# Attention followed by a mixture of experts: a hand-ordered attention phase, and mixing matmuls that write PSUM with a stride

## The chip, the cores and the metric

One core of one Trainium2 chip runs the whole program. The metric is the device time of one execution in microseconds (us), the median of three runs; a profile was taken of one further execution. Five engines work side by side: TensorE (PE, with its weight loads, PEld), VectorE (DVE), ScalarE (ACT), GpSimd (POOL) and SyncE (SP). POOL, SP and ACT also start DMA transfers.

## The reference, cut to what matters

```
P = sort_net                                  # [4, 8, 8, 8]; five row/column normalisations with exp
for _ in range(5):
    P = exp(P - max(P)); P = P / sum_rows; P = P / sum_cols
k_sorted = einsum('bhij,bhjcd->bhicd', P, k_blocks)   # 8 blocks of 96 rows, head size 64
v_sorted = einsum('bhij,bhjcd->bhicd', P, v_blocks)
x = softmax(q_block @ k_sorted_block.T / 8) @ v_sorted_block   # per block of 96 rows
logits = x @ w_gate + modality_bias[modality_id]       # x is [3072, 512], 8 experts
e = argmax(logits); gate = softmax(logits)[e]
out = gate * (relu(x @ w1[e]) @ w2[e])
```

q, k and v are [4, 8, 768, 64]; w1 is [8, 512, 1024] and w2 [8, 1024, 512], all float32 in memory and cast to bf16 by the DMA that loads them.

## The kernel before

The 32 pairs of batch and head are worked in two groups g of 16. In each group a partition holds one (head, block) pair, so that mixing the blocks by P is a matmul of a 128 x 128 slice of k or v with a block-diagonal matrix made of P (`bdk`, `bdv`). `sort_k` mixes 8 of the 96 key rows at a time (12 chunks a group), `sort_v` 4 of the 64 value columns (16 chunks a group); a chunk fills one PSUM bank with 512 float32 a partition, and one copy on DVE or ACT (L168, L175) casts it to bf16 and puts it into `kTb` (a part of `w_all`) or `v_sb`. There are two such banks (`mipsum`), which the q transposes share. In SBUF the mixed k is kept with the row c innermost, the mixed v with the column d innermost, while the chunk in PSUM has c or d outermost, so the copy writes single bf16 elements 192 or 130 bytes apart.

Group 0 is mixed first; then a loop over 32 units u (half a group's blocks of one head) does `expo(u)` on ACT, the scores matmuls of unit u+1, and `av(u)`, which ends on DVE with the normalised rows in `xb`. The 28 chunks of group 1 are mixed in units 2 to 15. Every eighth unit, 12 DMAs on SP's queue store `xb` to `x_scratch`. The order on each engine is made by a scheduler, which may move work that is written later ahead of work written earlier.

The tile `w_all` holds all eight experts' weights, 16 transfers of 1 MB on POOL's queue. Its regions for experts 3 to 7 first serve q, the mixed k, v and k, so a weight transfer has to wait until attention is done with its region.

After the loop comes the gate phase, 24 tiles of 128 rows (L333 to L367): ACT loads a tile of x, PE and DVE work out logits and ranks, ACT copies eight counts into `cnt_sb` (three buffers), and POOL's queue stores them to `cnt_scratch`. Then a short chain of small transfers makes offsets, 24 indirect DMAs scatter the row numbers (L434), and 31 slots run the expert matmuls (L443 to L484). One more transfer matters below: SP's `sidx_scratch<-dummy_t`, which fills a table with 3968 entries of 8 bytes as soon as DVE has set `dummy_t`.

Of the kernel before, what the change touches and what calls it, by code (L numbers as in the profile page):

```python
# [17 lines left out]
def kernel(  # L18
# [13 lines left out]
    nc = tc.nc  # L32
# [28 lines left out]
    KCH = 6  # L61
    KCW = BLK // KCH

    def load_k(g):
        for kc in range(KCH):
            raw = apool.tile([128, KCW * D], BF16, tag="k_raw", name=f"k_raw{g}_{kc}", bufs=2)
            nc.gpsimd.dma_start(out=raw, in_=k_src[g * 128:(g + 1) * 128, kc * KCW * D:(kc + 1) * KCW * D])
            rv = raw.rearrange("p (c d) -> p c d", d=D)
            for par in range(2):
                rows = slice(par * 64, (par + 1) * 64)  # L70
                nc.vector.tensor_copy(k_il[rows, kc * KCW:(kc + 1) * KCW, par], rv[rows])

# [3 lines left out]
    wpool = ctx.enter_context(tc.tile_pool(name="wpool", bufs=1))  # L76
    ph1 = ExitStack()
    apool = ph1.enter_context(tc.tile_pool(name="apool", bufs=3))
# [3 lines left out]
    mipsum = ph1.enter_context(tc.psum_pool(name="mipsum", bufs=2))  # L82

    P_t = singles.tile([BH, NB, NB], FP32)
    nc.sync.dma_start(out=P_t, in_=sort_net.rearrange("b h i j -> (b h) i j"))
    nc.vector.memset(k_il[0:64, :, 1], 0.0)
    nc.vector.memset(k_il[64:128, :, 0], 0.0)
    load_k(0)
    load_v(0)
    q_tiles = {}  # L90

    def load_q(g, hq):
        t = apool.tile([128, 2, 2, 6 * D], BF16, tag="q_in", name=f"q_in{g}_{hq}", bufs=2)
# [3 lines left out]
        il = apool.tile([128, 2, 6, 2, D], BF16, tag="q_il", name=f"q_il{g}_{hq}", bufs=2)  # L97
        for z in range(2):
            nc.vector.tensor_copy(il[:, z], t[:, :, z].rearrange("p r (t d) -> p t r d", d=D))
        q_tiles[g, hq] = il  # L100

    load_q(0, 0)
    load_q(0, 1)

    nc.vector.memset(v_in[:, BLK * D:128 * D], 0.0)
    v_sb = [a1.tile([128, 128, D + 1], BF16, tag=f"v_sb{gg}", name=f"v_sb{gg}") for gg in range(2)]
    for gg in range(2):
        nc.gpsimd.memset(v_sb[gg][:, :, D:D + 1], 1.0)
    attnT = [a1.tile([96, 8 * BLK + 32], BF16, tag=f"attnT{z}", name=f"attnT{z}") for z in range(3)]
    for z in range(3):  # L110
        nc.gpsimd.memset(attnT[z][:, 8 * BLK:], 0.0)
    ident = singles.tile([128, 128], BF16)
    make_identity(nc, ident)
# [4 lines left out]
    P_bf = singles.tile([BH, NB, NB], BF16)  # L118
    for it in range(5):
# [3 lines left out]
        nc.scalar.activation(P_t, P_t, ACT.Exp)  # L123
        nc.vector.tensor_reduce(red, P_t, AX.X, ALU.add)
# [8 lines left out]
    id3 = ident.rearrange("p (a j) -> p a j", j=NB)  # L133
    id3s = bass.AP(tensor=ident.tensor, offset=ident.offset,
                   ap=[ident.ap[0], [1, NB], [NB, 16]])
    jmask = singles.tile([128, NB], FP32)
    nc.vector.tensor_reduce(jmask, id3s, AX.X, ALU.add)
    bmask = singles.tile([128, 16], FP32)
    nc.vector.tensor_reduce(bmask, id3, AX.X, ALU.add)
    bd_v, bd_k = [], []  # L140
    for g in range(2):
        sel = singles.tile([BH, 16, NB], BF16, tag=f"sel{g}", name=f"sel{g}")
        nc.vector.tensor_copy(sel, ident[0:BH, g * 16:(g + 1) * 16].broadcast_to([BH, 16, NB]))
        rep = mipsum.tile([128, NB, NB], FP32, tag="mi", name=f"rep{g}")
        nc.tensor.matmul(rep.rearrange("p a b -> p (a b)"), sel.rearrange("p a b -> p (a b)"),
# [14 lines left out]

    v_cols = v_in.rearrange("p (c d) -> p d c", d=D)

    def sort_k(g, ch, act):
        acc = mipsum.tile([128, 8, 64], FP32, tag="mi", name=f"ka{g}_{ch}")
        for z in range(8):
            nc.tensor.matmul(acc[:, z], k_il[:, ch * 8 + z].rearrange("p r d -> p (r d)"), bd_k[g], start=True, stop=True)  # L166
        dst = kTb[g].rearrange("p (x c) -> p c x", c=BLK)[:, ch * 8:(ch + 1) * 8]
        (nc.scalar.copy if act else nc.vector.tensor_copy)(dst, acc)  # L168

    def sort_v(g, ch, act):  # L170
        acc = mipsum.tile([128, 4, 128], FP32, tag="mi", name=f"va{g}_{ch}")
# [12 lines left out]

# [66 lines left out]
    WLOAD = {14: 0, 18: 1, 22: 2}  # L251
# [62 lines left out]
    for e in range(3, E):  # L314
# [200 lines left out]
```

## Time and profile before

| | |
|---|---|
| Median of three runs | 630.01 us (629.17 to 630.42) |
| Profiled execution, its own time | 628.43 us |
| Span from first to last instruction in it | 626.3 us |
| Mean granted TensorE clock | 0.997 |
| Busy: PE, DVE, ACT, POOL | 277.0, 261.8, 192.7, 137.3 us |
| Loads from HBM, stores | 59.83 MB, 11.33 MB |

The span is shorter than the execution's own time by 2.1 us, which lie before the first and after the last instruction. Busy shares are averages over stages that have different limits, so each stage is read by itself below.

### The profile page before, as it was taken

To read this page: it belongs to the slowest core of one execution; us is meant where nothing else is said; L and a number is where in the kernel's file an instruction comes from. 1 tells how busy PE (TensorE), PEld (TensorE's weight loads), DVE (VectorE), ACT (ScalarE), POOL (GpSimd) and SP (SyncE) were. 2 spreads that over 40 slices of the span, in tenths; PEclk is the share of its full clock that TensorE was granted. 3 is DMA by queue.
4 is the path that set the end of the run, shared out by engine and by line. 5 is a ranking of instruction groups with operands and counts; after the bars stand their busy time and mean duration, and the time that the engine had idled before them with its cause. 6 is when DMAs were issued, how large, how long until landed. Compare 5 with 4: busy or idle time off the path is not lost.

```text
span 626.3 us, 6878 instructions
## 1 busy us (share of the span) xinstructions
PE 277.0 (44%) x2026; PEld 157.8 (25%) x2044; DVE 261.8 (42%) x769; ACT 192.7 (31%) x431; POOL 137.3 (22%) x180
## 2 busy tenths in 40 slices
PE   0002327653754406551000000068787886787775
PEld 0002225542532203331000000023333333333332
DVE  4438888878743506553000000023444343433342
ACT  0006775787332205551000000023333332333222
POOL 5311102110000101222222222122332332223222
PEclk9999999999999999999999999999999998999999
DMA  7999858793826593210000000011121121211210
GB/s 141 119 121 204 140 83 152 117 196 58 136 51 112 83 201 81 59 40 1 7 0 0 0 0 0 0 42 52 51 69 58 50 76 35 68 51 52 46 17 10
DMA packets 41337, 43.56 MB, mean 70 GB/s; under 512 B 14396, under 2 KB 32869, under 8 KB 41046
## 3 DMA queue, kind: packets, MB, share of 16 engines
q0 software_dynamic: 25184, 36.72, 31.6%
q1 hardware_dynamic: 12662, 3.26, 3.4%
q10 hardware_dynamic: 3456, 3.15, 2.2%
q8 instruction: 18, 0.29, 0.2%
q14 instruction: 17, 0.14, 0.1%
HBM read 59.83 MB, written 11.33 MB: 114 GB/s over the span
## 4 chain that ended last, share of the span: by engine, by line
DMA 29%; PE 27%; issue 16%; DVE 15%; ACT 8%; POOL 3%; SPq 1%; POOLq 0%; DVEq 0%; ACTq 0%
DMA sidx_scratch<-rg_all,dest_i_all 12%; PE h_p L462 8%; PE y_p L477 7%; DMA x_scratch<-xb 4%; PE hT_p L473 3%; ACT v_sb L175 3%; DVE v_sb L175 3%; DVE y_sb L481 3%; DMA x_t<-x_scratch,idxg 3%; DVE w_all L168 3%; DMA k_raw<-in_k_dram 3%; DMA q_in<-in_q_dram 2%; ACT w_all L168 2%; DMA out_dram<-y_sb,idxg 2%; PE va L173 2%
## 5 line engine op out<-in xcount | busy, mean ns | idle before, releaser
L456 PE MATMUL xT_p<-ident,x_t 128*128 128x128 bf16 x124 | 21.3, 221 | 141.2 <-DMA x_t<-x_scratch,idxg 123.4
L477 PE MATMUL y_p<-w_all,hT 128*128 x237 | 73.2, 379 | 0.6 <-ACT hT L474 0.6
L457 ACT COPY xT<-xT_p 128x128 bf16<-128x128 bf16 x62 | 16.5, 266 | 167.4 <-PE xT_p L456 167.4
L462 PE MATMUL h_p<-w_all,xT 128*128 x241 | 60.4, 391 | 9.9 <-issue 9.6
L450 POOL DMA_INDIRECT x_t<-x_scratch,idxg x31 | 30.5, 983 | 133.1 <-PE h_p L462 50.9
L457 DVE COPY xT<-xT_p 128x128 bf16<-128x128 bf16 x62 | 11.5, 217 | 111.3 <-PE xT_p L456 111.2
L473 PE MATMUL hT_p<-ident,h_sb 128*128 128x128 bf16 x248 | 49.6, 221 | 10.7 <-DVE hT L474 9.6
L474 DVE COPY hT<-hT_p 128x128 bf16<-128x128 bf16 x124 | 27.9, 225 | 46.6 <-PE hT_p L473 42.0
L456 PEld LDWEIGHTS <-x_t 128*128 128x128 bf16 x124 | 9.8, 97 | 144.1 <-DMA x_t<-x_scratch,idxg 127.0
L175 DVE CAST v_sb<-va 96x512 bf16<-96x512 f32 x16 | 39.1, 2445 | 10.2 <-PE va L173 10.1
L175 ACT CAST v_sb<-va 96x512 bf16<-96x512 f32 x16 | 39.3, 2454 | 12.5 <-PE va L173 12.5
L474 ACT COPY hT<-hT_p 128x128 bf16<-128x128 bf16 x124 | 32.8, 264 | 29.8 <-PE hT_p L473 26.1
L219 ACT ACTIVATE attnT<-sc 96x768 bf16<-96x768 f32 x32 | 26.8, 841 | 48.9 <-PE op L232 39.1
L467 DVE TENSOR_SCALAR h_sb<-h_p 128x512 bf16<-128x512 f32 x31 | 21.4, 692 | 47.5 <-PE h_p L462 47.5
L434 POOL DMA_INDIRECT sidx_scratch<-rg_all,dest_i_all x24 | 23.4, 974 | 75.7 <-DMA sidx_scratch<-rg_all,dest_i_all 71.3
L469 ACT ACTIVATE h_sb<-h_p 128x512 bf16<-128x512 f32 x31 | 18.5, 597 | 63.8 <-PE h_p L462 58.5
L482 POOL DMA_INDIRECT out_dram<-y_sb,idxg x31 | 31.4, 1014 | 25.9 <-DVE xT L457 13.2
L462 PEld LDWEIGHTS <-xT 128*128 128x128 bf16 x248 | 24.7, 99 | 46.3 <-issue 25.7
L168 ACT CAST w_all<-ka 128x512 bf16<-128x512 f32 x12 | 32.5, 2712 | 8.3 <-PE ka L166 8.3
L477 PEld LDWEIGHTS <-hT 128*128 128x128 bf16 x248 | 23.9, 96 | 44.0 <-issue 16.5
L481 DVE TENSOR_SCALAR y_sb<-y_p,idxg 128x512 f32<-128x512 f32 x31 | 23.3, 751 | 27.3 <-PE y_p L477 26.4
L236 DVE TENSOR_TENSOR xb<-op,rs 96x256 bf16<-96x256 f32 x64 | 26.0, 417 | 18.5 <-DMA x_scratch<-xb 16.9
(126 smaller groups left out, 450.4 us busy)
## 6 DMA issues: line engine op xcount, KB each, us to landing
w_all<-in_moe_w_dram POOLq DMA_DIRECT2D x16, 1024.0 KB, 12.2
k_raw<-in_k_dram POOLq DMA_DIRECT2D x12, 256.0 KB, 7.7
w_all<-in_v_dram POOLq DMA_DIRECT2D x2, 1536.0 KB
q_in<-in_q_dram POOLq DMA_DIRECT2D x16, 192.0 KB, 7.5
x_scratch<-xb SPq DMA_DIRECT2D x48, 64.0 KB, 6.1
x_t<-x_scratch ACTq DMA_DIRECT2D x24, 128.0 KB, 2.4
idxg<-sidx_scratch SPq DMA_DIRECT2D x31, 1.0 KB, 1.7
x_t<-x_scratch,idxg POOLq DMA_INDIRECT x31
```

The costliest lines, as they stand in the source:

```text
L168: (nc.scalar.copy if act else nc.vector.tensor_copy)(dst, acc)
L175: (nc.scalar.copy if act else nc.vector.tensor_copy)(dst, acc[0:BLK])
L219: nc.scalar.activation(attnT[u % 3][:, 0:8 * BLK].rearrange("p (r f) -> p r f", r=2), sc_tiles.pop(u)[0:BLK, :, 0:4 * BLK], ACT.Exp, scale ...
L450: nc.gpsimd.indirect_dma_start(out=x_t, out_offset=None, in_=x_dram, in_offset=bass.IndirectOffsetOnAxis(ap=idx[:, :1], axis=0))
L456: nc.tensor.transpose(xT_p, x_t[:, c * 128:(c + 1) * 128], ident)
L457: (nc.scalar.copy if c % 2 else nc.vector.tensor_copy)(xT[:, c], xT_p)
L462: nc.tensor.matmul(h_p, xT[:, c], w_all[:, bass.ds(e_sv * WCOL + c * F + half * 512, 512)], start=(c == 0), stop=(c == 3))
L473: nc.tensor.transpose(hT_p, h_sb[:, fc * 128:(fc + 1) * 128], ident)
L474: (nc.scalar.copy if fc % 2 else nc.vector.tensor_copy)(hT[:, fc], hT_p)
L477: nc.tensor.matmul(y_p, hT[:, fc], w_all[:, bass.ds(e_sv * WCOL + 4 * F + fc * Dm, Dm)], start=(fc == 0), stop=(fc == 7))
L481: nc.vector.tensor_scalar(y_sb, y_p, gate_t[:, 0:1], None, ALU.mult)
L482: nc.gpsimd.indirect_dma_start(out=out, out_offset=bass.IndirectOffsetOnAxis(ap=idx[:, :1], axis=0), in_=y_sb, in_offset=None, bounds_chec ...
```

## The change

The phase up to the end of the loop is put under `tc.manual_schedule()`, so that its instructions stay in the order in which they are written; later code may still be moved forward between them. The written order is new. `sort_k` and `sort_v` let each matmul write every 8th (or 4th) float32 of its bank, so that the copy reads PSUM in order and writes runs of 8 (or 4) bf16, 16 (or 8) bytes. A row of `v_sb` grows from 65 to 72 elements. k is loaded in three pieces, into the tile that later holds the mixed v of group 1, and half of the spreading of k and one clearing of it go from DVE to POOL. All copies of group 1 go to ACT. x gets two buffers, in the region of expert 2, whose weights move behind the loop. The masks are made inside the normalisation.

```diff
+    VW = D + 8
+    order = ExitStack()
+    order.enter_context(tc.manual_schedule())
+    k_raw = v_sb[1].rearrange("p x d -> p (x d)")[:, 0:BLK * D]
...
+    def spread_k(kc, par):
+        eng = nc.gpsimd if par else nc.vector
+        eng.tensor_copy(k_il[rows, kc * KCW:(kc + 1) * KCW, par],
+                        k_raw[rows, cs].rearrange("p (c d) -> p c d", d=D))
...
-        acc = mipsum.tile([128, 8, 64], FP32, tag="mi", name=f"ka{g}_{ch}")
+        acc = mipsum.tile([128, 64, 8], FP32, tag="mi", name=f"ka{g}_{ch}")
         for z in range(8):
-            nc.tensor.matmul(acc[:, z], k_il[:, ch * 8 + z].rearrange("p r d -> p (r d)"), bd_k[g], start=True, stop=True)
-        dst = kTb[g].rearrange("p (x c) -> p c x", c=BLK)[:, ch * 8:(ch + 1) * 8]
+            nc.tensor.matmul(acc[:, :, z], k_il[:, ch * 8 + z].rearrange("p r d -> p (r d)"), bd_k[g], start=True, stop=True)
+        dst = kTb[g].rearrange("p (x c) -> p x c", c=BLK)[:, :, ch * 8:(ch + 1) * 8]
...
-        acc = mipsum.tile([128, 4, 128], FP32, tag="mi", name=f"va{g}_{ch}")
+        acc = mipsum.tile([128, 128, 4], FP32, tag="mi", name=f"va{g}_{ch}")
         for z in range(4):
-            nc.tensor.matmul(acc[:, z], v_cols[:, ch * 4 + z], bd_v[g], start=True, stop=True)
-        dst = v_sb[g].rearrange("p x d -> p d x")[0:BLK, ch * 4:(ch + 1) * 4]
+            nc.tensor.matmul(acc[:, :, z], v_cols[:, ch * 4 + z], bd_v[g], start=True, stop=True)
+        dst = v_sb[g][0:BLK, :, ch * 4:(ch + 1) * 4]
...
     for n, (f, g, ch) in enumerate(sort_jobs[0]):
         f(g, ch, n % 2)
+        if n == 11:
+            load_k(1)
+            make_bd(1)
+    load_v(1)
+    load_q(0, 2)
+    load_q(0, 3)
...
-            x_tiles[g, hf] = apool.tile([BLK, 2, 4, H, D], BF16, tag="xb", name=f"xb{g}_{hf}", bufs=1)
+            x0 = 2 * WCOL + hf * 8 * Dm
+            x_tiles[g, hf] = w_all[0:BLK, x0:x0 + 8 * Dm].rearrange("p (r i h d) -> p r i h d", r=2, i=4, h=H)
...
-    WLOAD = {14: 0, 18: 1, 22: 2}
+    WLOAD = {14: 0, 19: 1}
...
         expo(u)
-        n = u + 1
-        if n < 32:
-            if (n // 8) % 2 == 0:
-                trans_q(n // 16, n % 8)
-            scores(n)
-        av(u)
-        if u >= 2 and u < 16:
+        if u + 1 < 32:
+            scores(u + 1)
+        prep_q(u + 2)
+        if u >= 2:
             for z in range(2):
                 if pend:
                     f, g, ch = pend.pop(0)
-                    f(g, ch, z)
+                    f(g, ch, 1)
+        av(u)
+    order.close()
     ph1.close()
-    for e in range(3, E):
+    for e in range(2, E):
         load_weights(e)
```

The first place is DVE where `dummy_t` is set, the tile that SP's fill of `sidx_scratch` waits for. Before, it stands ahead of the second of five normalisation sums (`red<-P_t`):

```order
L143 COPY sel_189<-ident 32x128
L263 TENSOR_TENSOR biasd<-biasd,bias_419 128x8
L267 MEMSET ones_col 128x1
L269 MEMSET dummy_t 128x62
L275 MEMSET zero_t 1x512
L270 MEMSET dummy_t 128x31
L71 COPY w_all<-k_raw_2_89 64x16x64 x2
L124 TENSOR_REDUCE red<-P_t 32x8
```

Now it stands behind DVE's last copy of group 0's mixed v (`va0_14`) and ahead of the first q tile:

```order
L196 CAST v_sb0_79<-va0_14_388 96x128x4
L288 TENSOR_TENSOR biasd_411<-biasd_411,bias0_409 128x8
L292 MEMSET ones_col_419 128x1
L294 MEMSET dummy_t_421 128x62
L295 MEMSET dummy_t_421 128x31
L300 MEMSET zero_t_425 1x512
L110 COPY q_il0_0_434<-q_in0_0_96 128x768 x2
```

The fill has moved from the normalisation to the end of group 0's mixing, which is also where POOL starts the load of group 1's v.

The second place is ACT in the loop, in units 3 to 5 (`sc` are scores, `ka1` chunks of group 1's k). Before, ACT has one chunk a unit and DVE the other:

```order
L219 ACTIVATE attnT0_123<-sc3_576 96x768
L168 CAST w_all_58<-ka1_1_611 128x8x64
L219 ACTIVATE attnT1_124<-sc4_630 96x768
L168 CAST w_all_58<-ka1_3_665 128x8x64
L219 ACTIVATE attnT2_125<-sc5_684 96x768
L168 CAST w_all_58<-ka1_5_719 128x8x64
```

Now ACT has both:

```order
L243 ACTIVATE attnT0_81<-sc3_540 96x768
L188 CAST w_all_58<-ka1_2_615 128x64x8
L188 CAST w_all_58<-ka1_3_625 128x64x8
L243 ACTIVATE attnT1_82<-sc4_598 96x768
L188 CAST w_all_58<-ka1_4_672 128x64x8
L188 CAST w_all_58<-ka1_5_682 128x64x8
```

DVE has no copy of group 1's chunks left.

The third place is POOL between the last weight transfers and the gate phase's count stores. Before:

```order
L253 DMA w_all<-in_moe_w_dram 128x4x1024
L397 IOTA iota_s 8x31
L367 DMA cnt_scratch<-cnt_sb 8x1x1 x24
L370 DMA cnt_2782<-cnt_scratch 24x8
L395 DMA padT_scratch<-padT_sb 8x1x1
```

Now two weight transfers, those of expert 2, stand behind the iota (which waits for the end of the loop), still ahead of the counts:

```order
L278 DMA w_all<-in_moe_w_dram 128x4x1024
L428 IOTA iota_s 8x31
L278 DMA w_all<-in_moe_w_dram 128x4x1024
L280 DMA w_all<-in_moe_w_dram 128x8x512
L398 DMA cnt_scratch<-cnt_sb 8x1x1 x24
L401 DMA cnt_2751<-cnt_scratch 24x8
```

Both before and now all 16 weight transfers stand ahead of the counts in POOL's queue.

## Rows read from the trace of the kernel before

**Rows 1.** The page, 40 slices of 15.7 us: busy tenths of the DMA engines.
```profile
DMA  7999858793826593210000000011121121211210
```

**Rows 2.** Chain of waits, 0 to 100 us: start us, length us, what.
```profile
24.73 15.69 DMA k_raw<-in_k_dram
...
49.36 0.62 PE ka L166 x8
...
71.67 2.43 DVE v_sb L175
...
74.76 2.43 DVE v_sb L175
...
96.78 1.46 PE tq L194 x12
```

**Rows 3.** Groups by line, 0 to 345 us: busy us, mean ns; idle ahead.
```profile
L175 DVE CAST v_sb<-va 96x512 bf16<-96x512 f32 x16 | 39.1, 2445 | 10.2 <-PE va L173 10.1
...
L168 DVE CAST w_all<-ka 128x512 bf16<-128x512 f32 x12 | 32.5, 2710 | 1.9 <-PE ka L166 1.8
```

**Rows 4.** Timeline of the loop, 188 to 207 us: start us, us, engine, line.
```profile
188.61 0.81 ACT L219 ACTIVATE attnT<-sc 96x768 bf16<-96x768 f32 x1 [0.83 <-PE op L232]
...
190.29 0.81 ACT L219 ACTIVATE attnT<-sc 96x768 bf16<-96x768 f32 x1 [0.88 <-PE op L232]
...
206.21 0.75 DVE L236 TENSOR_TENSOR xb<-op,rs 96x256 bf16<-96x256 f32 x2 [10.85 <-DMA x_scratch<-xb]
```

**Rows 5.** Timeline of POOL in the gate phase: 4th and 24th count store.
```profile
243.66 0.51 POOL L367 DMA_DIRECT2D cnt_scratch<-cnt_sb  x1 [1.58 <-ACT cnt_sb L366]
...
287.97 0.50 POOL L367 DMA_DIRECT2D cnt_scratch<-cnt_sb  x1 [1.38 <-ACT cnt_sb L366]
```

**Rows 6.** The page's costliest groups: two PSUM copies that write 512 elements in order.
```profile
L467 DVE TENSOR_SCALAR h_sb<-h_p 128x512 bf16<-128x512 f32 x31 | 21.4, 692 | 47.5 <-PE h_p L462 47.5
...
L469 ACT ACTIVATE h_sb<-h_p 128x512 bf16<-128x512 f32 x31 | 18.5, 597 | 63.8 <-PE h_p L462 58.5
```

**Rows 7.** Timeline of PE: k mixing, q transposes, an expert's 512-column matmuls.
```profile
63.41 1.01 PE L166 MATMUL ka<-bdk,w_all 128*128 128x64 bf16 x16 [2.38 <-DVE w_all L168]
...
98.69 0.82 PE L194 MATMUL tq<-ident,q_il 128*128 128x128 bf16 x6
...
426.68 1.89 PE L462 MATMUL h_p<-w_all,xT 128*128 x8 [0.28 <-issue]
```

**Rows 8.** Timeline of POOL at the start: clearing, and four load issues.
```profile
0.34 0.12 POOL L499 MEMSET const-uint8-127<- 128x1 uint8 x1
...
3.09 2.89 POOL L95 DMA_DIRECT2D q_in<-in_q_dram  x4
...
7.13 0.30 POOL masks.py:197 MEMSET ident<- 128x128 bf16 x1
```

**Rows 9.** DMA issues: count, KB each, median us from issue to landing.
```profile
w_all<-in_moe_w_dram POOLq DMA_DIRECT2D x16, 1024.0 KB, 12.2
k_raw<-in_k_dram POOLq DMA_DIRECT2D x12, 256.0 KB, 7.7
w_all<-in_v_dram POOLq DMA_DIRECT2D x2, 1536.0 KB
q_in<-in_q_dram POOLq DMA_DIRECT2D x16, 192.0 KB, 7.5
x_scratch<-xb SPq DMA_DIRECT2D x48, 64.0 KB, 6.1
...
sidx_scratch<-dummy_t SPq DMA_DIRECT2D x1, 31.0 KB, 16.2
```

**Rows 10.** Stretches of 6 us: busy PE, PEld, DVE, ACT, POOL; clock, DMA share, GB/s.
```profile
30.00:36.00 6.00, 0.00 (x0) 0.00 (x0) 0.00 (x0) 0.00 (x0) 0.00 (x0) 1.00 1.24 19
...
54.00:60.00 6.00, 1.01 (x16) 0.90 (x16) 5.71 (x4) 5.26 (x2) 1.67 (x3) 1.00 1.13 212
...
90.00:96.00 6.00, 2.26 (x16) 1.70 (x15) 4.84 (x4) 4.66 (x3) 0.58 (x1) 1.00 0.00 0
```

More of the change, by code (lines that the diff above doesn't have):

```diff
@@ L60 @@
     v_src = v.rearrange("b h (n c) d -> (b h n) (c d)", n=NB)
-    KCH = 6
+    KCH = 3
     KCW = BLK // KCH
[L64 to L71, printed above, removed]
-    def load_v(g):
-        nc.gpsimd.dma_start(out=v_in[:, 0:BLK * D], in_=v_src[g * 128:(g + 1) * 128])
+    VW = D + 8
     wpool = ctx.enter_context(tc.tile_pool(name="wpool", bufs=1))
     ph1 = ExitStack()
-    apool = ph1.enter_context(tc.tile_pool(name="apool", bufs=3))
+    apool = ph1.enter_context(tc.tile_pool(name="apool", bufs=2))
     a1 = ph1.enter_context(tc.tile_pool(name="a1", bufs=1))
@@ L96, in load_q, with spread_q @@
                                 .rearrange("h (p t) d -> p h (t d)", t=6))
-        il = apool.tile([128, 2, 6, 2, D], BF16, tag="q_il", name=f"q_il{g}_{hq}", bufs=2)
+        q_raw[g, hq] = t
+    def spread_q(g, hq):
+        t = q_raw.pop((g, hq))
+        il = apool.tile([128, 2, 6, 2, D], BF16, tag="q_il", name=f"q_il{g}_{hq}")
         for z in range(2):
@@ L100, in load_q @@
         q_tiles[g, hq] = il
+    nc.vector.memset(k_il[0:64, :, 1], 0.0)
+    make_identity(nc, ident)
+    load_k(0)
+    load_v(0)
     load_q(0, 0)
     load_q(0, 1)
[L105 to L109, printed above, removed]
+    nc.gpsimd.memset(k_il[64:128, :, 0], 0.0)
+    nc.gpsimd.memset(v_in[:, BLK * D:128 * D], 0.0)
+    for kc in range(KCH):
+        spread_k(kc, 1)
+    nc.gpsimd.memset(v_sb[0][:, :, D:D + 1], 1.0)
     for z in range(3):
         nc.gpsimd.memset(attnT[z][:, 8 * BLK:], 0.0)
-    ident = singles.tile([128, 128], BF16)
-    make_identity(nc, ident)
+    jmask = singles.tile([128, NB], FP32)
+    bmask = singles.tile([128, 16], FP32)
+    sel = [singles.tile([BH, 16, NB], BF16, tag=f"sel{g}", name=f"sel{g}") for g in range(2)]
     red = singles.tile([BH, NB], FP32)
@@ L123 @@
         nc.scalar.activation(P_t, P_t, ACT.Exp)
+        if it == 0:
+            nc.vector.tensor_reduce(jmask, id3s, AX.X, ALU.add)
+        elif it == 1:
+            nc.vector.tensor_reduce(bmask, id3, AX.X, ALU.add)
+            for g in range(2):
+                nc.vector.tensor_copy(sel[g], ident[0:BH, g * 16:(g + 1) * 16].broadcast_to([BH, 16, NB]))
+        else:
+            spread_k(it - 2, 0)
         nc.vector.tensor_reduce(red, P_t, AX.X, ALU.add)
@@ L131, with make_bd @@
         nc.vector.tensor_tensor(P_bf if it == 4 else P_t, P_t, colb, ALU.mult)
[L133 to L139, printed above, removed]
     bd_v, bd_k = [], []
-    for g in range(2):
-        sel = singles.tile([BH, 16, NB], BF16, tag=f"sel{g}", name=f"sel{g}")
-        nc.vector.tensor_copy(sel, ident[0:BH, g * 16:(g + 1) * 16].broadcast_to([BH, 16, NB]))
+    def make_bd(g):
         rep = mipsum.tile([128, NB, NB], FP32, tag="mi", name=f"rep{g}")
-        nc.tensor.matmul(rep.rearrange("p a b -> p (a b)"), sel.rearrange("p a b -> p (a b)"),
+        nc.tensor.matmul(rep.rearrange("p a b -> p (a b)"), sel[g].rearrange("p a b -> p (a b)"),
                          P_bf.rearrange("p a b -> p (a b)"), start=True, stop=True)
@@ L285, with prep_q @@
     mod_words = mod_h.bitcast(I32).ap().rearrange("(t w) -> t w", w=256)
-    load_q(0, 2)
-    load_q(0, 3)
-    trans_q(0, 0)
+    def prep_q(u):
+        if u < 32 and (u // 8) % 2 == 0:
+            if u % 2 == 0:
+                spread_q(u // 16, (u % 8) // 2)
+            trans_q(u // 16, u % 8)
+    prep_q(0)
+    prep_q(1)
     scores(0)
@@ L293 @@
     for u in range(32):
-        if u == 0:
-            load_k(1)
-            load_v(1)
+        if u < 3:
+            spread_k(u, 1)
+            spread_k(u, 0)
+        if u == 3:
+            nc.gpsimd.memset(v_sb[1][:, :, D:D + 1], 1.0)
         if 9 <= u <= 12:
```

37 lines of the change are left out of this document (24 added, 13 removed).

## The prediction

> **What bounds the kernel now.** I read the page's 40 slices first, because the engines' shares are averages over stages. The DMA row [rows 1] is high but uneven up to slice 15 (about 235 us) and thin afterwards: first attention, under which the weights are loaded, then the gate phase, which sends its last count store at 288 us [rows 5], then the scatter and the experts. What the change touches lies in the first, so the question is when the gate phase can finish.
>
> The chain of waits names two things in attention. Group 0's mixing cannot start before 49.4 us, because k's third piece lands only at 40.4 us after a wait of 15.7 us [rows 2]. In 30 to 36 us the DMA engines are fully busy and move 19 GB/s, against 212 in a stretch of large loads [rows 10]: that is SP's fill in 8-byte pieces, 16.2 us to landing [rows 9]. Then the chain alternates between mixing matmuls and copies. A v copy ends at 74.10 us and the next on that bank's turn begins at 74.76 [rows 2], so a turn is 0.66 us of PE and hand-over plus a copy of 2.45 (v) or 2.71 us (k) [rows 3]. The 28 chunks of group 0 last until q's transposes begin at 96.8 us [rows 2]. Further on, a unit that neither mixes nor transposes takes 1.68 us (190.29 - 188.61), and one waits 10.9 us for the stores that read its only x buffer [rows 4]. While copies hold regions, no load can start: 90 to 96 us moves nothing [rows 10].
>
> **The change, part by part.** *The copies.* A copy that writes 512 elements in order takes 0.69 us on DVE, 0.60 on ACT [rows 6]; one that writes 512 single elements takes 2.71, or 5.3 ns each, and v's 4.8 [rows 3]. The new ones write 64 runs (k) or 128 (v). The bounds are 0.6 us and, if shorter runs bought nothing, 2.7. If the price belongs to each separate place, 64 x 5.3 = 0.34 and 128 x 4.8 = 0.61 us are covered by the streaming time, so I take 0.69. A turn is then 0.66 + 0.69 = 1.35 us for two banks, 0.68 us a chunk.
>
> The Trainium skill ("Vector Engine (DVE) Microarchitecture Reference", 5.2 Measured stream behaviour) says that a DVE port keeps its full rate where runs are at least two adjacent 4-byte words from an 8-byte boundary; by it both copies stream. No row of before has such runs. Its sum would be this one; the opposite bound would leave the mixing as it is.
>
> *The matmuls.* PE now writes every 8th or 4th float32. No row shows such a write. From below it costs nothing; from above, what single places cost the copies: 5.3 and 4.8 ns a column, 2.7 and 2.45 us a chunk. What is there to hide it: eight 512-column matmuls take 1.89 us, 0.46 ns a column, while 16 k matmuls of 64 columns take 1.01 us, 0.99 ns a column, and so are not set by their columns [rows 7]. A column could cost twice as much unseen. I take nothing, the end near the only matmul rows there are.
>
> The Trainium skill ("PSUM — Partial Sum Buffer", Specifications (TRN2)) speaks against this: PSUM has 8-byte lines, and any access that is not contiguous "slows matmuls significantly". It gives no factor; its case is the rival that ends slower, below.
>
> *Start.* The fill is off the normalisation, so k's pieces follow each other and have landed by about 14 us (1.6 MB at 212 GB/s, 7.5 us, behind issues that now end at 6.0 [rows 8]). From landing to first mixing took 49.4 - 40.4 = 9 us [rows 2], and most normalisation steps now run before the last piece lands; that gives 18 to 23 us. POOL gets new work: its issues, with one more for k and the identity ahead of them, run to about 7.5; then it clears 6144 + 2048 elements a partition and spreads 2048 three times. Clearing 128 elements takes 0.30 us against 0.12 for one [rows 8], 1.4 ns an element: 11.5 us, and 2.9 for each spread. First mixing at 22 us (18 at 1 ns, 31 at 2.3), k's last spread at 28, its mixing done at 31, the second mask 1, v 16 x 0.68 = 11: group 0 is done at **43 us** instead of 97.
>
> *The new stall.* The fill now starts at 42 to 43 us, just as POOL starts group 1's v (1.6 MB), with q for heads 4 to 7 behind it. It holds the DMA engines 16 us, as before; then 2 MB at 212 GB/s take 9. So q lands at about 68 us. Units 0 and 1 are over by 51. In unit 2 DVE waits for that q, PE for its transpose, and PE, in written order, holds back the first chunk of group 1 and `av(2)`: a stall of about 17 us.
>
> *The loop.* To the 1.68 us of a plain unit I add PE's work: two chunks 2 x 0.5 (units 2 to 15), a transpose 0.8 (units 2 to 5 and 14 to 21) [rows 7]; ACT's 0.81 [rows 4] + 2 x 0.6 stays under that. Units 2 to 15: 14 x 2.7 + 6 x 0.8 = 42 us, so unit 16 at 110; the rest 16 x 1.68 + 6 x 0.8 = 32: the loop ends at **142**. The second x buffer removes the waits for stores.
>
> *The DMA engines become the bound.* Weights 16.8 MB and k, v, q and x stores at 3.15 each [rows 9] are 29.4 MB. Of these k twice, v and a quarter of q, 5.5, are moved before the fill, so 23.9 MB remain at 42 us: 113 us at 212 GB/s. Between 70 and 110 us only the rest of q and the four weight transfers whose regions are free by then can move, 5.5 MB, 27 of 40 us: 13 us idle. Last weight at 42 + 16 + 113 + 13 = **184 us**, long after the loop. All 16 stand in POOL's queue ahead of the counts, and a small transfer behind large ones on a queue waits, as k's piece did. ACT has three count buffers, so tile 3 of the gate phase waits until count 0 has landed, at 185.5. From the fourth count store to the last took 287.97 - 243.66 = 44.3 us [rows 5]: the gate phase ends at 230 instead of 288.
>
> *The rest.* Scatter and experts keep order and work: 626.3 - 288.0 = 338.3 us. Sum 230 + 338.3 = 568, plus the 2.1 us outside the span: 570, against 628.43 of the profiled execution. The median shown is 1.6 higher, hence **571 us**.
>
> **The rivals.** *Slower: the strided writes cost PE what single places cost the copies.* A chunk is then 2.6 us of PE: group 0 takes 73 us, ending at 95; the fill stall follows to 118; units 2 to 15 take 14 x (1.68 + 5.2) + 5 = 101, unit 16 at 219, weights 74 us behind it as above, 293; gate phase 339; total 681. It decides from about 1.75 us a chunk, 3.4 ns a column, where last weight comes at 243. For it: nothing shows the write. Against: it needs seven times the 0.46 ns. 5 in 100.
>
> *Half the gain in mixing*: copies of 1.3 us, or columns of 2 ns, add some 0.3 us a chunk of group 0 and 0.5 a unit or more: 16 us, of which the idle of the DMA queue takes half: 580. For it: no row has runs of 8 or 16 bytes. 14 in 100.
>
> *The counts get past the weights*, because they need only their own few bytes: then the program's own waits hold only tile 10, 14 tiles of 2.2 us follow the last weight, 184 + 31 = 215, total 557. Against: the late k piece. 10 in 100.
>
> *The fill holds nothing up*: it shares the engines with larger pieces; 16 us less, 555. Against: 19 GB/s beside waiting loads. 9 in 100.
>
> *No change within 0.2%*, about what a measurement of this kernel can tell from none: some mixture of late weights; 1 in 100.
>
> **How the numbers follow.** The forecast, with POOL's start and the load rate as bounds (1 ns an element: 4 us less; 2.3: 9 more; 190 instead of 212 GB/s: 13 more), spans 558 to 590 and has 61 in 100. The range of 8 in 10 takes in the two quicker rivals and the half gain: 548 to 600. Faster 94, same 1, slower 5.
>
> **What would show it.** The copies of k and v at 0.6 to 0.7 us, PE's chunks still near 0.5; first mixing near 22 us, group 0 done near 43; a gap of all engines in unit 2 that a q load ends; the loop's end near 142; then ACT waiting in the gate phase for a count store, up to the last weight near 184; scatter and experts as long as before. Wrong would make it: PE chunks above 1.5 us, POOL's spreads above 5 us, weights that land well before the loop's end, or counts that land while weights still move.

## The result, and the profile after

The changed kernel takes **560.47 us** (median of 4 runs, 558.72 to 562.56) against 630.21 of the kernel before on the same chip: a ratio of 0.8896, with a 95% interval of 0.8864 to 0.8929. The time lies inside the forecast range and 11 us below the forecast of 571. The profiled execution is one of 558.72 us with a span of 556.9.

The page first: the granted clock, the busy share of the DMA engines and what they moved, in 40 slices of 13.9 us.

```profile
PEclk9997599555555555555555555999999999998998
DMA  6928999999995220000000001111111111111110
GB/s 128 211 59 141 59 210 222 224 220 231 224 228 92 57 49 1 8 0 0 0 0 0 0 0 29 48 57 58 58 57 54 57 58 58 57 59 57 30 23 1
```

From the sixth to the twelfth slice (70 to 167 us) the DMA engines move 210 to 231 GB/s without a gap; in [rows 1] the same stage was uneven and lasted to about 235 us. The clock row has a long stretch at half, of which more at the end.

Groups by line, 0 to 250 us: shapes and count, then busy us, mean ns of one, and the idle time ahead of them with what ended it.

```profile
L196 ACT CAST v_sb<-va 96x512 bf16<-96x512 f32 x24 | 14.3, 653 | 9.2 <-PE va L193 9.1
...
L188 ACT CAST w_all<-ka 128x512 bf16<-128x512 f32 x18 | 10.4, 592 | 26.9 <-PE ka L185 26.9
...
L196 DVE CAST v_sb<-va 96x512 bf16<-96x512 f32 x8 | 5.5, 686 | 5.0 <-PE va L193 5.0
...
L188 DVE CAST w_all<-ka 128x512 bf16<-128x512 f32 x6 | 4.2, 692 | 5.3 <-PE ka L185 5.3
...
L397 ACT COPY cnt_sb<-cnt_p 1x8 f32<-1x8 f32 x24 | 3.7, 156 | 8.6 <-DMA cnt_scratch<-cnt_sb 8.6
...
L357 DVE CAST mod<-modraw 24x128 bf16<-24x128 int32 x1 | 0.2, 214 | 20.9 <-DMA modraw<-in_moe_modality_id_dram 20.9
```

The copies of [rows 3] now cost what the in-order copies of [rows 6] cost. The last two rows are waits that did not matter before: ACT waits once, 8.6 us, for a count store (before, no count waited), and DVE waits 20.9 us for 24 KB of modality ids (before, 1.5 us).

Two chunks of k's mixing on PE, from the timeline (1.01 us in [rows 7]):

```profile
28.39 1.05 PE L185 MATMUL ka<-bdk,w_all 128*128 128x64 bf16 x16 [0.33 <-DVE w_all L188]
```

The chain of waits, its pieces named by start and length:

```profile
23.10 4.52 PE ka L185 x40
...
46.47 11.95 DMA q_in<-in_q_dram
...
95.71 12.09 DMA q_in<-in_q_dram
...
135.00 4.66 DMA x_scratch<-w_all
139.67 6.22 DMA x_scratch<-w_all
```

Mixing starts at 23.1 us where [rows 2] had 49.4. Behind group 0's mixing, whose copies are in the chain with 0.7 us each, it passes through loads and stores. The timeline of POOL shows where the stage ends (first, third, fourth and 24th count store):

```profile
150.81 0.57 POOL L398 DMA_DIRECT2D cnt_scratch<-cnt_sb  x1 [3.47 <-ACT xT L372]
...
158.86 0.50 POOL L398 DMA_DIRECT2D cnt_scratch<-cnt_sb  x1 [2.23 <-ACT cnt_sb L397]
173.54 0.51 POOL L398 DMA_DIRECT2D cnt_scratch<-cnt_sb  x1 [14.18 <-ACT xT L372]
...
217.30 0.50 POOL L398 DMA_DIRECT2D cnt_scratch<-cnt_sb  x1 [1.38 <-ACT cnt_sb L397]
```

The 24th store, at 287.97 us in [rows 5], comes at 217.30: 70.7 us earlier. What follows takes 556.9 - 217.3 = 339.6 us, against 338.3 before. So the whole gain lies ahead of the scatter, and between the third and the fourth store lies a hole of 14.7 us: the weights stand ahead of the counts on POOL's queue, and experiment 6 shows that this is its cause.

### The profile page after: what moved, and what is told of

Read it like the earlier page. It is cut to its first block, busy times and chain, and to the rows that moved or that the text cites. A ratio compares the mean times of both kernels' runs of the same rounds, so it can differ in the third digit from the quotient of the medians.

```text
span 556.9 us, 6871 instructions
## 1 busy us (share of the span) xinstructions
PE 272.3 (49%) x2044; PEld 157.0 (28%) x2044; DVE 199.5 (36%) x735; ACT 143.9 (26%) x445; POOL 154.0 (28%) x182
## 4 chain that ended last, share of the span: by engine, by line
PE 35%; DMA 28%; issue 19%; DVE 12%; POOL 4%; ACT 1%; POOLq 0%; SPq 0%; ACTq 0%; DVEq 0%
DMA sidx_scratch<-rg_all,dest_i_all 14%; PE h_p L493 10%; PE y_p L508 10%; DMA q_in<-in_q_dram 4%; PE hT_p L504 4%; DVE y_sb L512 4%; PE ka L185 3%; PE va L193 2%; POOL cnt_scratch L398 2%; DMA x_scratch<-w_all 2%; DMA x_t<-x_scratch 2%; DMA x_t<-x_scratch,idxg 2%; DMA v_sb<-in_k_dram 1%; PE op L257 1%; DVE w_all L261 1%
## 5 line engine op out<-in xcount | busy, mean ns | idle before, releaser
L487 PE MATMUL xT_p<-ident,x_t 128*128 128x128 bf16 x124 | 21.7, 221 | 140.1 <-DMA x_t<-x_scratch,idxg 121.7
L508 PE MATMUL y_p<-w_all,hT 128*128 x248 | 75.9, 379 | 0.0
L493 PE MATMUL h_p<-w_all,xT 128*128 x248 | 62.9, 399 | 9.0 <-issue 8.1
L508 PEld LDWEIGHTS <-hT 128*128 128x128 bf16 x248 | 23.9, 96 | 44.2 <-issue 16.5
L371 PE MATMUL xT_p<-ident,x_t 128*128 128x128 bf16 x96 | 19.9, 278 | 28.0 <-ACT xT L372 15.2
L398 POOL DMA_DIRECT2D cnt_scratch<-cnt_sb x24 | 12.1, 506 | 58.3 <-ACT cnt_sb L397 40.7
L261 DVE TENSOR_TENSOR w_all<-op,rs 96x256 bf16<-96x256 f32 x64 | 26.9, 421 | 2.3
L504 PEld LDWEIGHTS <-h_sb 128*128 128x128 bf16 x248 | 20.8, 98 | 15.4 <-DVE h_sb L498 14.2
```

Source lines behind the costliest of these rows:

```text
L261: nc.vector.tensor_tensor(xb[:, par, :, h], op[0:BLK, :, 0:D], rs.broadcast_to([BLK, 4, D]), ALU.mult)
L487: nc.tensor.transpose(xT_p, x_t[:, c * 128:(c + 1) * 128], ident)
L493: nc.tensor.matmul(h_p, xT[:, c], w_all[:, bass.ds(e_sv * WCOL + c * F + half * 512, 512)], start=(c == 0), stop=(c == 3))
L504: nc.tensor.transpose(hT_p, h_sb[:, fc * 128:(fc + 1) * 128], ident)
L508: nc.tensor.matmul(y_p, hT[:, fc], w_all[:, bass.ds(e_sv * WCOL + 4 * F + fc * Dm, Dm)], start=(fc == 0), stop=(fc == 7))
```

## Experiments

All ratios are to the kernel before, run on the same chip. The reading that matters most in each trace is the time of the 24th count store ("the gate's end"): 287.97 us before, 217.30 after. It is a finer measure than the total: the work behind it is the same in both kernels and in all experiments but the eleventh, and takes 336.3 to 343.9 us in their traces, so a difference of 3 or 4 us between two totals says little. The theory: cheap copies and the early start turn the stage from one bound by copies into one bound by the DMA engines, which show as weights that hold the counts. Rivals: one half of the change (layout, or order and start) carries it all; the strided PSUM access costs something; the fill makes the stall.

**1. The layout alone.** In the kernel before, only `sort_k`, `sort_v` and the row of `v_sb` (72 instead of 65 elements) take the new layout.

```diff
-        acc = mipsum.tile([128, 8, 64], FP32, ...)
+        acc = mipsum.tile([128, 64, 8], FP32, ...)
-            nc.tensor.matmul(acc[:, z], k_il..., bd_k[g], ...)
+            nc.tensor.matmul(acc[:, :, z], k_il..., bd_k[g], ...)
-        dst = ...rearrange("p (x c) -> p c x", c=BLK)[:, ch * 8:(ch + 1) * 8]
+        dst = ...rearrange("p (x c) -> p x c", c=BLK)[:, :, ch * 8:(ch + 1) * 8]
```

> The kernel before, with nothing changed but the layout of the mixing (every 8th or 4th float32 of PSUM written by the matmuls, copies that write runs of 16 or 8 bytes, rows of v_sb of 72 elements). Theory, that cheap copies are the larger part and that the end of the gate phase follows the DMA engines once they are cheap: copies of 0.6 to 0.7 us, group 0's mixing from 49 to about 72 us instead of 97, the gate phase's last count store at about 243 instead of 288, 585 us in all (570 to 600). Rival, that the written order and the earlier start carry the gain and the copies are hidden by what else is waited for: 615 to 630 us with the same short copies.

Measured: 587.05 us, ratio 0.9327 (0.9282 to 0.9371). One row by line, and POOL's 24th count store:

```profile
L175 DVE CAST v_sb<-va 96x512 bf16<-96x512 f32 x16 | 11.0, 686 | 8.7 <-PE va L173 8.6
```

```profile
242.08 0.50 POOL L367 DMA_DIRECT2D cnt_scratch<-cnt_sb  x1 [1.38 <-ACT cnt_sb L366]
```

The gate's end comes at 242.1 us, 45.9 earlier than before. The layout alone is worth 43 of the 70 us.

**2. Everything but the layout.** The reverse: in the changed kernel the lines of the layout go back, for k and likewise for v; only the longer rows of `v_sb` stay.

```diff
-        acc = mipsum.tile([128, 64, 8], FP32, ...)
+        acc = mipsum.tile([128, 8, 64], FP32, ...)
-            nc.tensor.matmul(acc[:, :, z], k_il..., bd_k[g], ...)
+            nc.tensor.matmul(acc[:, z], k_il..., bd_k[g], ...)
-        dst = ...rearrange("p (x c) -> p x c", c=BLK)[:, :, ch * 8:(ch + 1) * 8]
+        dst = ...rearrange("p (x c) -> p c x", c=BLK)[:, ch * 8:(ch + 1) * 8]
```

> The changed kernel with the old layout of the mixing alone put back (PSUM written in order, copies that write single bf16 elements). Theory: copies of 2.4 to 2.7 us again; group 0 done at about 69 us instead of 44; in units 2 to 15 ACT has 0.81 + 2 x 2.7 = 6.2 us a unit instead of about 2, so the loop ends near 190 and the last count store comes near 257 instead of 217: 600 us (590 to 615). Rival, that the DMA queue sets the end anyway and hides the copies: 560 to 572 us.

Measured: 626.9 us, ratio 0.9938 (0.9907 to 0.9969); the gate's end at 284.6 us. This is far from the rival and well above my 600. Groups by line, 0 to 300 us:

```profile
L196 ACT CAST v_sb<-va 96x512 bf16<-96x512 f32 x24 | 56.5, 2504 | 7.0 <-PE va L193 6.9
L188 ACT CAST w_all<-ka 128x512 bf16<-128x512 f32 x18 | 48.3, 2807 | 18.8 <-PE ka L185 18.7
```

and POOL's count stores, the third, the fourth and the 24th:

```profile
228.41 0.50 POOL L398 DMA_DIRECT2D cnt_scratch<-cnt_sb  x1 [2.15 <-ACT cnt_sb L397]
240.84 0.51 POOL L398 DMA_DIRECT2D cnt_scratch<-cnt_sb  x1 [11.93 <-ACT xT L372]
...
284.64 0.50 POOL L398 DMA_DIRECT2D cnt_scratch<-cnt_sb  x1 [1.38 <-ACT cnt_sb L397]
```

Group 0 was done at 69 us and the loop ended near 191, both as expected. But ACT's copies kept the regions of the weights, 12 of the 16 transfers were issued after 160 us, and the counts waited for them: the fourth store came 2.8 us earlier than that of [rows 5], and from there on the kernel is the one before. The gains of the two halves are 45.9 and 3.3 us at the gate's end, 49.2 in sum; together they are 70.7. The other 21.5 us come only when both are there. My reading is that an early start is worth something once the copies no longer sit on ACT and on the weights' regions.

**3. Which side of the copy costs.** The matmuls write PSUM in order again and the copy reads it with the stride; its runs of 16 and 8 bytes stay.

```diff
+            nc.tensor.matmul(acc[:, z], k_il..., bd_k[g], ...)      # acc is [128, 8, 64]
+        src = acc.rearrange("p c x -> p x c")
```

> The changed kernel, but with the matmuls writing PSUM in order and the copies reading it with the stride (every 64th or 128th float32); the copies still write the same runs of 16 or 8 bytes. Theory, that the price of the old copy was that of its single 2-byte writes and neither PE's nor the copy's stride in PSUM costs anything: copies of 0.6 to 0.7 us, same time as the changed kernel, 560 us within 3. Rival, that it was the pair of layouts, so that a copy that jumps in PSUM is slow too: copies of 1.3 to 2.7 us and 575 to 600 us. Second rival, that PE's strided writes did cost something hidden: PE's 16 k matmuls under 1.0 us and 2 to 5 us less in all.

Measured: 556.77 us, ratio 0.8851 (0.8806 to 0.8896), which overlaps that of the changed kernel. PE's mixing of two chunks, from the timeline, and two copies by line:

```profile
24.45 1.01 PE L185 MATMUL ka<-bdk,w_all 128*128 128x64 bf16 x16 [0.36 <-DVE w_all L188]
```

```profile
L188 ACT CAST w_all<-ka 128x512 bf16<-128x512 f32 x18 | 10.3, 586 | 23.8 <-PE ka L185 23.6
...
L188 DVE CAST w_all<-ka 128x512 bf16<-128x512 f32 x6 | 4.2, 692 | 4.0 <-PE ka L185 4.0
```

The stride may stand on either side of PSUM. A copy that reads every 64th float32 takes the same 0.69 us, and PE's 16 matmuls take 1.01 us instead of 1.05 in the changed kernel. The old price was that of single 2-byte writes into SBUF. The rival that PE's strided writes cost something hidden is not borne out either: the median is 3.7 us lower, but the gate's end comes at 217.67 us, no earlier than the 217.30 of the changed kernel, so the 3.7 us do not come from the mixing. The Trainium skill ("PSUM — Partial Sum Buffer", Specifications (TRN2)) says that any access that is not contiguous slows matmuls significantly; here the difference is 0.04 us in 1.05, so at these widths and strides it is not seen. The rows can't exclude a small cost: these matmuls take 0.99 ns a column in order where the experts' 512-column ones take 0.46 [rows 7], so about half a nanosecond a column could stay hidden.

**4. The written order.** One line is taken out; the scheduler then orders the same code.

```diff
-    order.enter_context(tc.manual_schedule())
```

> The changed kernel without the manual order: same layout, same code, but the scheduler puts the instructions in its own order (the fill moves ahead again, POOL's loads change places). Theory, that the hand order is worth something but less than the copies: 575 us (565 to 590), lost where a load waits behind another. Rival, that the order is worth nothing beside the layout: within 3 us of 560. Rival, that it carries the larger part: over 595 us.

Measured: 550.49 us, ratio 0.8731 (0.8689 to 0.8773): 10 us *faster* than the changed kernel, on the side that I had given to no theory. POOL's 24th count store, SP's fill, and the page's GB/s:

```profile
210.70 0.50 POOL L397 DMA_DIRECT2D cnt_scratch<-cnt_sb  x1 [1.38 <-ACT cnt_sb L396]
```

```profile
13.90 0.40 SPq L297 DMA_DIRECT2D sidx_scratch<-dummy_t  x1
```

```profile
GB/s 143 137 112 149 156 208 223 227 227 230 222 216 50 57 31 0 8 0 0 0 0 0 0 0 29 58 59 53 54 58 55 59 59 62 64 52 59 29 21 1
```

Mixing starts 4.4 us later here and group 0's last copy ends at 55.8 us instead of 44.2, and still the gate's end comes 6.6 us sooner. The fill runs under the first loads, the next q is asked for at 28 us instead of 46, the first weight at 45 instead of 66; the third and fifth slice carry 112 and 156 GB/s where the changed kernel has 59 and 59. The hand order starts the engines sooner and the loads later, in a stage that the DMA engines bound. Which of the moved loads carries the gain was not tried apart. Nor was what brings this kernel 37 us below the layout alone (587.05): the three loads of k, POOL's share of the spreading, the second x buffer and the copies of group 1 on ACT stand in both it and the changed kernel, and no run takes one of them away. In the trace of experiment 1 the loop still waits 16.9 us for stores that read its only x buffer, and mixing begins at 48.7 us.

**5 to 8. The four suspects of the DMA-bound stage, one at a time.** The lines are cut short, with the number of the experiment in front and comments added.

```diff
5+    sidx_fill = ... ap=[[2 * NS, 128], [2, NS], [1, 2]]      # was [[2, 128], [256, NS], [1, 2]]
6+        nc.sync.dma_start(out=cnt_dram[t:t + 1], in_=cnt_sb)  # was nc.gpsimd
7+            load_weights(0); load_weights(1)                  # behind load_k(1); WLOAD gone
8+        t = apool.tile([128, 2, 2, 6 * D], BF16, tag="q_in", ..., bufs=4)
```

> The changed kernel with the fill of sidx_scratch written in 128 runs of 248 bytes in place of 3968 pieces of 8 bytes (every entry has the same value, so what is in memory stays the same). Theory, that the pieces slow the loads beside them and so cause the stall of unit 2: the fill lands within 4 us, the DMA engines keep above 190 GB/s from 48 to 60 us, unit 2's q comes about 2 us and the next q 6 us earlier, and 6 us less in all: 554 (550 to 558). Rival, that the stall is only v and q in line behind each other, or that the end hangs on the last weight alone, whose 16 transfers are not moved: 560 us within 2.

Measured: 560.47 us, ratio 0.8868 (0.8831 to 0.8905): no change. Issues by line (KB, us to landing), and DVE's first use of unit 2's q:

```profile
sidx_scratch<-dummy_t SPq DMA_DIRECT2D x1, 31.0 KB, 12.0
```

```profile
57.51 1.17 DVE L110 COPY q_il<-q_in 128x768 bf16<-128x768 bf16 x2 [3.51 <-DMA q_in<-in_q_dram]
```

The fill lands after 12.0 us instead of 23.8, and unit 2's q comes at 57.5 instead of 58.5 us; the gate's end, at 215.0, is 2.3 us earlier. The stall stays. I read it from the order of POOL's queue: v of group 1 (1.5 MB) stands ahead of that q and lands at 56.1 us here, 12.2 us after its issue, and at 56.5, after 12.3, in the changed kernel. The rival holds so far as the time goes; that it is the weights' place that sets the time is what 6 and 8 show.

> The changed kernel with the 24 count stores of the gate phase issued by SP instead of POOL, so that they do not stand behind the weights in POOL's queue. Theory, that they wait for the weights because they share their queue: ACT's wait of 8.6 us for a count store goes, tile 3 follows tile 2 in about 2.5 us, the last count store comes near 206 instead of 217, 550 us (546 to 554). Rival, that a small store waits for the weights on any queue, because the DMA engines are full: the fourth count store still at 172 or later and 560 us within 2.

Measured: 553.65 us, ratio 0.8759 (0.8716 to 0.8801). ACT's fourth count, 7.9 us earlier than the same copy in the changed kernel (173.10), with no wait ahead of it, and its last:

```profile
165.18 0.15 ACT L397 COPY cnt_sb<-cnt_p 1x8 f32<-1x8 f32 x1
...
209.90 0.15 ACT L397 COPY cnt_sb<-cnt_p 1x8 f32<-1x8 f32 x1
```

The counts wait because they share POOL's queue with the weights, not because the DMA engines are full. The last count is copied at 209.9 us, some 7 us sooner, not the 11 I gave: beside the weights a tile takes (209.90 - 150.67) / 23 = 2.58 us instead of 2.2.

> The changed kernel with the weights of experts 0 and 1, whose regions hold nothing before, loaded right behind k of group 1 (issued from about 23 us) instead of in units 14 and 19. Theory, that the last weight sets the end and the DMA engines are half idle from 23 to 45 us: 4.2 MB go there, the last weight lands near 158 instead of 172, and the last count store near 206: 549 us (543 to 555), in spite of v and q of units 0 to 3, which stand behind these weights and come 5 to 12 us later. Rival, that the loop, later by that much, sets the end: 560 to 570 us.

Measured: 557.8 us, ratio 0.8827 (0.8783 to 0.887): the gate's end at 213.7 us, and a time not told apart from the changed kernel's. Unit 2's q, and the first and fourth count store:

```profile
66.58 0.63 DVE L110 COPY q_il<-q_in 128x768 bf16<-128x768 bf16 x2 [12.22 <-DMA q_in<-in_q_dram]
```

```profile
158.39 0.57 POOL L399 DMA_DIRECT2D cnt_scratch<-cnt_sb  x1 [3.55 <-ACT xT L373]
...
169.56 0.51 POOL L399 DMA_DIRECT2D cnt_scratch<-cnt_sb  x1 [1.58 <-ACT cnt_sb L398]
```

The wait at the fourth count is gone, as the theory has it, but q comes 8 us later and the gate phase starts 7.6 us later. One wait was traded for another: the loop and the weights end close together.

> The changed kernel with four q_in buffers instead of two, so that q of group 1 is issued ahead of the weights of POOL's queue and not among them. Theory, that the loop hides under the weights: the third stall (PE idle from 102 to 108 us, ACT's wait of 6.4 us) goes and the loop ends near 118 instead of 124, but the last weight still lands near 172 and the time stays at 560 within 2. Rival, that the loop's end carries the gate phase: 554 us (552 to 556).

Measured: 560.88 us, ratio 0.8868 (0.8824 to 0.8912): no change. ACT's first count that waits:

```profile
171.76 0.15 ACT L397 COPY cnt_sb<-cnt_p 1x8 f32<-1x8 f32 x1 [14.41 <-DMA cnt_scratch<-cnt_sb]
```

The first count store is 7.6 us earlier (143.2 us) and ACT then waits 14.4 us instead of 8.6 for the same weight; the fourth store comes at 172.2 us instead of 173.5 and the gate's end at 215.9. Of 7.6 us 1.4 are left there: this is the cleanest proof that the loop's end was not the bound.

**9 and 10. Suspects together.** The ninth kernel has edits 5, 6 and 8; the tenth has edits 6 and 8 without the manual order.

> The changed kernel with three of the single edits together: count stores issued by SP, four q_in buffers, the fill in 248-byte runs. Theory, that with the counts past the weights the loop's end sets the gate phase, so that the earlier q loads, worth nothing alone, now count: gate phase begins 7 us earlier, last count store near 202, 545 us (541 to 549). Rival, that the weights still hold the gate phase by slowing its x_t loads: no better than the counts alone, 552 to 555 us.

Measured: 543.48 us, ratio 0.8633 (0.8593 to 0.8674). Against experiment 6 the ratio falls by another 0.0126, some 8 us. The earlier q and the shorter fill, worth nothing alone, count as soon as the counts have left the weights' queue; which of the two carries the 8 us was not tried apart.

> The kernel without the manual order, with count stores issued by SP and four q_in buffers. Theory, as for the last: its loop ends near 112 instead of 119, the gate phase's last count store near 198 instead of 211: 540 us (535 to 546). Rival, that this order gains nothing from the count queue because its last weight comes with the loop's end anyway: 548 to 551 us.

Measured: 541.65 us, ratio 0.8592 (0.8555 to 0.8629), not told apart from the ninth. With counts and q mended the two orders come out alike, but the tenth lacks edit 5, so they differ in the fill too. Both end the loop near 114 us and start the gate phase only at 136 to 137. The trace of the ninth says why:

```profile
136.54 0.21 DVE L357 CAST mod<-modraw 24x128 bf16<-24x128 int32 x1 [19.66 <-DMA modraw<-in_moe_modality_id_dram]
```

The 24 KB of ids stand behind 48 x stores on SP, and PE's and ACT's first work of the phase stands behind them.

**11 and 12. The next wait.** Both have edits 5, 6 and 8. The eleventh moves besides the weights of experts 2 to 7 behind the loop, the ids ahead of it, and the small transfers ahead of the scatter to SP; the twelfth is the ninth with the ids early and nothing else. The diff is cut short, with comments added.

```diff
+    modraw = wpool.tile([NT, 256], I32, tag="modraw")    # 11 and 12: ahead of the loop
+    nc.sync.dma_start(out=modraw, in_=mod_words)
...
+    for e in range(2, E):                                # 11 only: inside the manual order
+        load_weights(e)
     order.close()
     ph1.close()
-    for e in range(2, E):
-        load_weights(e)
...
+    nc.sync.dma_start(out=cnt24, in_=cnt_dram)           # 11 only; so six more small transfers
```

> The changed kernel with the counts on SP, four q_in buffers, the fill in 248-byte runs, the small transfers between gate phase and scatter on SP too, and the weights of experts 2 to 7 behind the loop in POOL's queue, the first of them waiting for the last x stores; the small load of the modality ids comes early. Theory, that the weights slow the loop's q loads, its x stores and the gate phase's start, and are themselves not needed until the experts, some 100 us later: loop ends near 112, gate phase begins near 122 instead of 147, last count store near 182, weights landed by 200, ahead of most of the scatter: 527 us (518 to 540). Rival, that the scatter's transfers wait behind the weights on POOL's queue so that the weights set the end again: 540 to 555 us.

Measured: 539.72 us, ratio 0.8544 (0.8496 to 0.8591). The gate phase begins at 119.8 us and its last count is copied at 187.2, but the loop ends at 117 and not at 112. The weights still run when the seven small transfers between counts and scatter do: from the load of the counts (191.55) to the first scatter (214.69) 23.1 us, against 16.9 in the ninth. Neither expectation holds whole. That the weights cost these 6 us is a reading: the DMA engines move 202 GB/s in 200 to 205 us and 17 in 205 to 210, and no run takes the weights away.

> The three edits of the run before last (counts on SP, four q_in buffers, fill in 248-byte runs) and the 24 KB load of the modality ids issued before the loop instead of behind the 48 x stores on SP; nothing else. Theory, that with the counts past the weights the gate phase's start is held by this one small load (PE's first transpose of the phase stands behind the one that needs it, and waited 21 us there): gate phase begins at about 119 instead of 137, 24 tiles at 2.6 us, last count store near 183 instead of 201, 527 us (520 to 534). Rival, that the first tiles then wait for x stores and x_t loads under the weights just as long: 538 to 544 us.

Measured: 539.57 us, ratio 0.8574 (0.8542 to 0.8606), where I had 527; the ratio's interval overlaps that of the ninth. The phase does begin at 118.9 us, and its first tiles wait for x_t loads, the first 5.5 us, as the rival has it. The larger wait is another one. ACT's fourth count, and the rows of SP's queue:

```profile
154.90 0.15 ACT L397 COPY cnt_sb<-cnt_p 1x8 f32<-1x8 f32 x1 [10.72 <-DMA cnt_scratch<-cnt_sb]
```

```profile
108.01 41.45 SPq L269 DMA_DIRECT2D x_scratch<-w_all  x24
149.83 48.61 SPq L398 DMA_DIRECT2D cnt_scratch<-cnt_sb  x24
```

The counts now stand behind the x stores on SP as they stood behind the weights on POOL, which neither expectation names. The place is the same and the wait is not. On POOL the first three stores had been issued by 158.86 us and stood among the queue's transfers behind the weights; the longest took 14.5 us from issue to landing, where the median is 1.9. On SP the first store was issued only at 149.83 us, once SP had issued the last x store (108.01 + 41.45 = 149.46), and landed 5.05 us later. The last four kernels, 540 to 543 us, beat both kernels of this case by some 3% and 14%; which of them is best the intervals do not settle.

## Why the prediction was right, and where it was not

*The copies* (0.69 us on DVE, 0.60 on ACT): 0.69 and 0.59 to 0.65. The rule of the Trainium skill that the prediction set beside it ("Vector Engine (DVE) Microarchitecture Reference", 5.2 Measured stream behaviour: full rate for runs of two words from an 8-byte boundary) agrees with the 692 and 686 ns. The table of the same section, taken on SBUF tiles, gives 1.73 ns a column for a source that hops 4 KiB at every element, where adjacent ones take 1.05. It does not speak of PSUM; experiment 3 hops 256 bytes at every float32 of PSUM and stays at 692 ns for 512, the time of a copy in order.

*The strided PSUM writes* (nothing): 1.05 us for 16 matmuls, 1.01 without the stride. The slower rival, 681 us, needed 2.6 us a chunk.

*The start* (22 us) and *group 0* (43 us): 23.1 and 44.2. The first is right by luck, for the prediction hangs it on POOL and the trace on DVE:

```profile
23.10 4.96 PE L185 MATMUL ka<-bdk,w_all 128*128 128x64 bf16 x48 [1.12 <-DVE bdk L175]
```

PE waits for `bdk`, the end of DVE's normalisation, when POOL's spreads have been over since 20.9 us. Two errors cancel: POOL's clearing takes 0.85 ns an element (5.22 us for 6144) and not 1.4, and a spread 2.2 us and not 2.9, while DVE lost about 6.6 us to POOL (last section), which I did not foresee.

*The stall in unit 2*: named rightly as the place where a q load is waited for, wrong in cause and size. I put 17 us and an end at 68 us on the fill. The q lands at 58.5 us and PE waits 6.7 us; experiment 5 takes half of the fill's time to landing away and moves q by 1 us. What holds q is, by the order of the queue, v ahead of it.

*The loop* (end at 142 us): 125, the end of DVE's last product. I added PE's terms to the unit of [rows 4] where they overlap. In units 6 to 13 a unit takes 1.65 us, the spacing of ACT's exponentials (77.24, 78.89, 80.53), not 2.7. A later wait of 6.4 us, for group 1's q behind weights, was not foreseen; experiment 8 shows that it costs nothing.

*The DMA engines become the bound, and the counts wait for the last weight*: right, and shown by experiments 6 and 8. The size is off: the weights land near 171.5 us and not at 184, and the fourth count is stored at 173.1 to 173.5 and not at 185.5. I had written off 29 us, 16 for the fill and 13 of idle. From 42 to 70 us the DMA engines move 2.9 MB (76, 161 and 47 GB/s in 42 to 48, 48 to 60 and 60 to 70 us), which at my 212 GB/s is 13.5 of the 28 us, so some 14.5 were lost and the term was some 14 us too long, about what the weights come early. *The gate phase from the fourth count on* (44.3 us) took 43.8, and *the rest* (338.3) 339.6: with the fourth store 12.0 us early, that makes the 11 us by which the forecast is too long. The ground that I gave for the wait, k's late piece, was weak: in [rows 10] that piece stood beside SP's fill on another queue, and not behind large loads on its own. Experiment 6 is what shows the wait in the queue.

*The rival that the counts get past the weights* (557) does not hold for this kernel, yet it is what experiment 6 builds, at 553.65. *The rival that the fill holds nothing up* (555) is half right: experiment 5 halves the fill's time to landing, the gate's end comes only 2.3 us earlier and the time does not change; the loss that it would save lay partly elsewhere. What I missed altogether is the load of the ids: 20.9 us of wait at the start of the gate phase, hidden behind the wait for the weights and worth nothing until that one is gone.

## What to carry to other kernels

When a phase has been cut, ask which queue its first small transfer stands in, and behind what: here counts behind weights, ids behind x stores, and then counts behind x stores held an engine of the next phase for 9 to 21 us each. Two edits that are worth 46 and 3 us alone can be worth 71 together, and one that is worth nothing alone can be worth several when another wait is gone, so test them together before dropping one. For a transposing copy like these (float32 in PSUM, strides of 16 to 512 bytes), give the SBUF side the runs and let PSUM take the stride.

## What the runs showed of the hardware beyond that

DVE's copies and products wait whole instructions of POOL out. Timeline of DVE while POOL clears and spreads:

```profile
9.15 3.43 DVE L91 COPY w_all<-v_sb 64x2048 bf16<-64x2048 bf16 x1 [0.93 <-DMA v_sb<-in_k_dram]
...
12.96 0.21 DVE L152 TENSOR_TENSOR P_t<-P_t,red 32x64 f32<-32x64 f32 x1
...
15.24 1.44 DVE L152 TENSOR_TENSOR P_t<-P_t,red 32x64 f32<-32x64 f32 x1
...
17.23 1.29 DVE L157 TENSOR_TENSOR P_t<-P_t,red 32x64 f32<-32x64 f32 x1
18.45 0.67 DVE L91 COPY w_all<-v_sb 64x2048 bf16<-64x2048 bf16 x1
```

and of POOL:

```profile
6.81 5.22 POOL L119 MEMSET w_all<- 64x6144 bf16 x1
...
14.39 6.50 POOL L91 COPY w_all<-v_sb 64x2048 bf16<-64x2048 bf16 x3
```

The same copy takes 3.43 us when it starts within POOL's clearing, and ends 0.55 us after that (12.58 against 12.03); the one at 18.45 takes 0.67. The small product takes 0.21 us, at 12.96 even beside a clearing of POOL (12.09 to 14.32), but 1.44 and 1.29 while POOL copies. The reductions and reciprocals between them keep their 0.19 to 0.25 us. The excess over these rows and their like is 2.8 + 0.3 + 2 x 1.2 + 1.1 = 6.6 us, on the path to the first mixing. The Trainium skill ("SBUF — State Buffer", SBUF: two separate sides) says that DVE and GpSimd share a port pair, held for a whole instruction: by a GpSimd operation against a DVE operation in a two-port mode, and against one with two SBUF inputs only where GpSimd's reads SBUF. The trace agrees for the products, which POOL's copies hold up and its clearing does not; no row says in which mode the held copy ran.

The granted clock was 0.50 (the level of 1.2 GHz) from 48 to about 72 us and from 96 us until the experts had begun, elsewhere 1.00 (2.4 GHz). Ahead of the first fall PE had been busy 7.7 us of the 12 from 36 to 48, ahead of the second 3.8 of the 6 from 90 to 96. Before, and in the second experiment, it stayed near 1.00 through this stage. The times do not follow it: 20 count stores take 43.8 us at 0.50 and took 44.3 at 1.00, since that phase waits on hand-overs and loads; only where PE has a queue of work is it seen, as in 16 mixing matmuls that take 1.91 us at 59.54 us and 1.05 at full clock.
